# Decode attention backward: whole-head stores move from GpSimd to ScalarE, and o and dq leave in small parts

## The chip, the cores and the metric

The kernel runs on one core of one Trainium2 chip. A core has five engines with a queue of instructions each: TensorE (PE in the profile; its weight loads are PEld), VectorE (DVE), ScalarE (ACT), GpSimd (POOL) and SyncE (SP), which here only issues DMAs. Sixteen DMA engines move data between the HBM and the core's SBUF. The time is device microseconds of one execution; the figure given for a kernel is the median of its runs. A profile is one further execution, and its span runs from the first instruction to the last.

## The reference: what is computed

Attention with one query per head, forward and backward, for 64 heads (batch 2 x 32), 8192 keys and head size 128, all in bfloat16:

```python
scores = jnp.einsum("bhqd,bhkd->bhqk", q, k) * scale
p = _softmax(scores, axis=-1)
return jnp.einsum("bhqk,bhkd->bhqd", p, v)
...
_out, _vjp = jax.vjp(_f, q, k, v)
_grads = _vjp(grad_out)
```

Results are o (out_0), dq (out_1), dk (out_2) and dv (out_3). With dS the gradient of the scores, dk is an outer product of dS and q, and dv one of p and grad_out. So for every head the kernel reads K and V, 2 MB each, and writes dk and dv, 2 MB each; o and dq are 16 KB for all heads together.

## The kernel before

K or V of a head is one tile, [128, 64, 128], with 64 key rows of 256 bytes, one after another, in each of 128 partitions: a transfer of 128 runs of 16 KB. SBUF holds twelve such tiles, six heads. dv of a head is written over its V tile and dk over its K tile, in place; when the tile has been stored, a tile of the head six later is loaded into it. `slot_of` (L80) swaps the two kinds: K of head i + 6 goes where V of head i was, since V is done first.

The program is one long, unrolled list. The loop at L487 goes over slots, eight per head (`SL`), and each slot holds steps of up to four heads. In slot r of a head (`at` and `within` pick the head for which a step is due):

- r = 0 to 7: `transpose_chunk` (L213) turns 16 key rows with eight TensorE transposes into one of two PSUM buffers (`tp`, L220), and ScalarE copies them out (`ev`, L222); r = 0 to 3 for K, 4 to 7 for V. One slot later `score_chunk` (L225) multiplies the copy by the query's window (`raw`, L241). The windows are written by ScalarE (`window`, L194) in slots 1 and 5.
- r = 4 to 12: the score rows are spread over the partitions, the maximum is taken, the exponential (ScalarE, L303) and the sums follow.
- r = 8 to 11 and 12 to 15: `acc` (L390) accumulates o and dq on TensorE.
- r = 9 to 12: `outer` (L450) writes dv into the V tile, a quarter a slot (VectorE, L456); r = 13 to 16: the same for dk.

When `outer` has written the last quarter, it issues the store (L474), on GpSimd, whose DMAs are software DMAs (queue q0 in the profile): GpSimd itself writes their descriptors. For the last head each quarter is stored by itself, on SP. Five heads (6, 18, 30, 42, 54; `SPREAD`) have their K tile stored in two pieces, of 126 partitions and of 2 (`by_rows`, L85). One slot after a store of V, and one after a store of K, the loop calls `load` (L92) for the tile of the head six later; loads go out on SP, as hardware DMAs (queue q1).

`pin` keeps each engine's instructions in the order in which the code writes them. Waits are not written by hand: the framework gives each instruction the semaphores that it must wait for, and each DMA a semaphore that it raises when it has landed. A DMA's wait is made by the engine that issues it, in its place in that engine's queue.

At the start q and grad_out are loaded (L116), the first six rows of q by GpSimd (L112). At the end (L558 to L563) dq and then o, both gathered in SBUF with one column per head, are transposed, copied by VectorE (`nat`, L562) and stored on SP with one DMA each.

Of the kernel before, what the change touches and what calls it, by code (L numbers as in the profile page):

```python
# [11 lines left out]
BF16 = mybir.dt.bfloat16  # L12
# [6 lines left out]
SG = 4  # L19
SW = 32  # L20
NTILE = 12
FIRST = 6
SPREAD = range(6, 60, 12)

@with_exitstack
def kernel(
# [11 lines left out]
    nc = tc.nc  # L39
    B, H, Sq, D = q.shape  # L40
    Sk = k.shape[2]
    P = nc.NUM_PARTITIONS
    assert Sq == 1 and D == P
    BH = B * H
    assert BH <= P
    NT = Sk // P
    assert NT * P == Sk and NT % CH == 0
    NCH = NT // CH
# [1 line left out]
    scale = float(D) ** -0.5  # L50

    load_eng = nc.sync
    store_eng = nc.gpsimd
    pin = tc.keep_in_program_order

    const = ctx.enter_context(tc.tile_pool(name="const", bufs=1))
# [6 lines left out]
    ps_m = ctx.enter_context(tc.tile_pool(name="ps_m", bufs=1, space=bass.MemoryType.PSUM))  # L63
# [12 lines left out]
            self.qb = [None, None]  # L76

    heads = [Head() for _ in range(BH)]

    def slot_of(i, w):  # L80

        n = 2 * i + w
        return n if n < NTILE else slot_of(i - NTILE // 2, 1 - w)

    def by_rows(eng, dst, src, rows):  # L85

        p = 0
        for m in rows:
            pin(eng.dma_start(out=dst[p : p + m], in_=src[p : p + m], max_dma_last_dim=NT * D))
            p += m  # L90

    def load(i, w, pieces=(NCH,)):  # L92
        h = heads[i]
        t = kvp.tile([P, NT, D], BF16, tag=f"kv{slot_of(i, w)}", name="kvt")
        h.tile[w] = t
        src = (v_v if w else k_v)[i]
        c = 0
        for m in pieces:
            n0, n1 = c * CH, (c + m) * CH
            pin(load_eng.dma_start(out=t[:, n0:n1, :], in_=src[:, n0:n1, :]))  # L100
            c += m
# [3 lines left out]
    qd_nat = evp.tile([P, CH, P], BF16, tag="ev", name="qd_nat")  # L105
    for w, a in enumerate((q, grad_out)):
        rows = a.rearrange("b h s d -> (b h s) d")
        r0 = FIRST if w == 0 else 0
        if r0:
            pin(store_eng.inc_swdge_sem([], [], mode="reset_dge_cursor"))  # L110
            pin(
                store_eng.dma_start(  # L112
                    out=qd_nat[:r0, w, :], in_=rows[:r0], max_dma_last_dim=D
                )
            )
        pin(load_eng.dma_start(out=qd_nat[r0:BH, w, :], in_=rows[r0:BH]))  # L116

    load(0, 1)
    for j in range(1, min(NTILE // 2, BH)):
# [22 lines left out]
    for g in range(SG):  # L142
        nc.vector.tensor_copy(
            out=sel4[g * SW : (g + 1) * SW, :, g // 2, :],
            in_=ident_f[g * SW : (g + 1) * SW, g * SW : g * SW + 2 * NCH].rearrange(
                "p (c t) -> p c t", t=2
            ),
# [9 lines left out]
    for w in range(2):  # L157
        nc.vector.tensor_copy(
            out=qd_pair[:BH, w],
            in_=qd_nat[:BH, w, :]  # L160
# [4 lines left out]
        for e in range(2):  # L165
            tps = ps_m.tile([P, BH], BF16, tag=f"acc{e}", name="tps")
# [8 lines left out]
    for w in range(2):  # L175
        tps = ps_m.tile([P, BH], BF16, tag=f"acc{w}", name="tps")
# [3 lines left out]
    dqT = const.tile([P, BH], BF16)  # L180
    oT = const.tile([P, BH], BF16)

    def begin(i):

        h = heads[i]
        sw = ps_sdp.tile([P, 2 * NT + 2 * P + 4], F32, tag="s", name="sw")
        h.score = (sw[:, 0:NT], sw[:, NT : 2 * NT])
        h.s, h.dp = h.score
        h.mT = sw[0:1, 2 * NT : 2 * NT + P]
        h.qbp = sw[:, 2 * NT + P : 2 * NT + 2 * P]  # L190
        h.lsum = sw[:, 2 * NT + 2 * P : 2 * NT + 2 * P + 2]
        h.mb = sw[:, 2 * NT + 2 * P + 2 : 2 * NT + 2 * P + 3]

    def window(i, w):  # L194

        pin(nc.scalar.copy(out=qwin[:, w, :, Q0 : Q0 + 2], in_=qpair[:, w, i]))
# [16 lines left out]
    def transpose_chunk(i, c):  # L213
        w, c = divmod(c, NCH)
        src = heads[i].tile[w]
        tp = ps_tp.tile([P, CH // 2, P], F32, tag="tp", name="tp")
        for m in range(CH // 2):
            n0 = c * CH + 2 * m
            two = src[:, n0 : n0 + 2, :].rearrange("p n d -> p (n d)").bitcast(F32)
            pin(nc.tensor.transpose(tp[:, m, :], two, ident_f[:]))  # L220
        ev = evp.tile([P, CH // 2, P], F32, tag="ev", name="ev")
        pin(nc.scalar.copy(out=ev[:], in_=tp[:]))  # L222
        return ev
# [226 lines left out]
    def outer(i, w, c, ends):  # L450

        h = heads[i]
        n0 = c * CH
        shape = [P, CH, D // 2, 2]
        pin(
            nc.vector.tensor_tensor(  # L456
                out=h.tile[w][:, n0 : n0 + CH, :].rearrange("p n (e t) -> p n e t", t=2),
                in0=h.qb[w][:]
                .rearrange("p (e t) -> p e t", t=2)
                .unsqueeze(1)  # L460
                .to_broadcast(shape),
                in1=h.pair[w][:, n0 : n0 + CH, :].unsqueeze(2).to_broadcast(shape),
                op=ALU.mult,
            )
        )
        if c + 1 in ends:
            at = ends.index(c + 1)
            b0, b1 = (ends[at - 1] if at else 0) * CH, (c + 1) * CH
            dst = (dv_v if w else dk_v)[i]
            if w == 0 and i in SPREAD:  # L470
                by_rows(store_eng, dst, h.tile[w], (P - 2, 2))
            else:
                eng = load_eng if len(ends) > 1 else store_eng
                pin(eng.dma_start(out=dst[:, b0:b1, :], in_=h.tile[w][:, b0:b1, :]))  # L474

    A1 = NCH + 4
    O1 = A1 + 1
    A0 = A1 + NCH
    O0 = A0 + 1
    whole = [NCH]  # L480
    last = list(range(1, NCH + 1))
    AHEAD = NTILE // 2
# [4 lines left out]
    for g in range(SL * BH + O0 + NCH + 4 - SL):  # L487
        now = [(g // SL - b, g % SL + b * SL) for b in range(4)]
        now = [(i, r) for i, r in now if 0 <= i < BH]

        def at(r0):

            return next((i for i, r in now if r == r0), None)

        def within(r0):

            return next(((i, r - r0) for i, r in now if r0 <= r < r0 + NCH), None)

        if (i := at(O1 + NCH)) is not None and i + AHEAD < BH:
            load(i + AHEAD, 0)  # L500
        if (i := at(O0 + NCH)) is not None and i + AHEAD < BH:
            load(i + AHEAD, 1)
        if x := within(O1):
            outer(x[0], 1, x[1], last if x[0] == BH - 1 else whole)
        if x := within(O0):
            outer(x[0], 0, x[1], last if x[0] == BH - 1 else whole)
        ev = None
        if g < SL * BH:
            i, r = divmod(g, SL)
            if r == NCH:  # L510
                begin(i)
                broadcast(i, 1)
            if r == NCH + 2:
                broadcast(i, 0)
            ev = transpose_chunk(i, r)
        if (i := at(A1 + NCH + 2)) is not None:
            join(i, 1)
        if (i := at(A0 + NCH + 2)) is not None:
            join(i, 0)
        if x := within(A1):  # L520
            acc(x[0], 1, x[1])
        if x := within(A0):
            acc(x[0], 0, x[1])
        if (i := at(NCH + 1)) is not None:
            spread_rows(i, 0)
        if (i := at(SL + 1)) is not None:
            spread_rows(i, 1)
        if (i := at(NCH + 3)) is not None:
            max_spread(i)
            expo(i)  # L530
        if prev is not None:
            score_chunk(*prev)
        prev = (g // SL, g % SL, ev) if ev is not None else None
        if (i := at(NCH + 1)) is not None and i + 1 < BH:
            window(i + 1, 0)
        if (i := at(1)) is not None and i > 0:
            window(i, 1)

        if (i := at(NCH)) is not None:
            keep_raw(i)  # L540
        if (i := at(SL)) is not None:
            keep_raw(i)
        if (i := at(NCH + 1)) is not None:
            max_part(i)
        if (i := at(NCH + 2)) is not None:
            max_all(i)
        if (i := at(NCH + 4)) is not None:
            normalise_p(i)
        if (i := at(SL + 1)) is not None:
            weigh(i)  # L550
        if (i := at(SL + 2)) is not None:
            normalise_ds(i)
        if (i := at(A1 + NCH)) is not None:
            pick(i, 1)
        if (i := at(A0 + NCH)) is not None:
            pick(i, 0)

    for w, (src, dst) in enumerate(((dqT, out_1), (oT, out_0))):  # L558
        tps = ps_m.tile([BH, P], BF16, tag=f"acc{w}", name="tps")
        nc.tensor.transpose(tps[:], src[:], ident_bf)  # L560
        nat = evp.tile([P, CH, P], BF16, tag="ev", name="nat")
        nc.vector.tensor_copy(out=nat[:BH, 0, :], in_=tps[:])  # L562
        load_eng.dma_start(out=dst.rearrange("b h s d -> (b h s) d"), in_=nat[:BH, 0, :])  # L563

# [28 lines left out]
```

## Time and profile before

| what | us |
|---|---|
| median of 3 runs (lowest, highest) | 1272.13 (1270.76, 1272.67) |
| the profiled execution: span, which is all that it gives of its own time | 1270.2 |
| TensorE busy in it | 1189.4 (94%) |
| VectorE busy | 1030.9 (81%) |
| ScalarE busy | 557.0 (44%) |
| GpSimd busy | 72.9 (6%) |
| HBM read and written | 268.47 MB each, 423 GB/s over the span |
| issues of SP: tile loads of 2 MB | 127, about 20 to landing (median) |
| issues of GpSimd: whole stores of 2 MB | 121, 49.3 to landing (median) |

How to read it: "busy" counts the time in which an engine executes, and engines work side by side, so shares don't add up to one. "To landing" is the time from a DMA's issue to its completion, queueing included. The page also has the span in 40 equal slices, with the busy share of each engine in tenths, the mean busy share of the DMA engines and what they moved; a list of DMA queues; and a list of waits, which puts each wait of an engine down to what ended it.

### The profile page before, as it was taken

The page shows a single profiled execution, that of the slowest core. Times are in us where ns is not written, and L with a number is a line of the kernel's source. Part 1 is how long each engine was busy: PE and PEld are TensorE (multiplying, and loading weights), DVE is VectorE, ACT ScalarE, POOL GpSimd, SP SyncE. Part 2 cuts the span into 40 slices and gives each one's busy share as a digit, 9 for nine tenths or more (in the row PEclk, how much of TensorE's full clock was granted, in tenths as well). Part 3 has the DMA queues.
Part 4 walks back from the last instruction along what each step waited for, and adds up shares of the span by engine and source line. Part 5 has one row for each costly group of instructions (what it writes and reads, how often), then busy time and mean ns, then how long its engine had stood idle before and what let it go on. Part 6 is the DMA issues. An engine that isn't in the chain of part 4 may idle for free.

```text
span 1270.2 us, 24551 instructions
## 1 busy us (share of the span) xinstructions
PE 1189.4 (94%) x10056; PEld 784.5 (62%) x10056; DVE 1030.9 (81%) x2267; ACT 557.0 (44%) x769; POOL 72.9 (6%) x138
## 2 busy tenths in 40 slices
PE   6999999999999999999999999999999999999991
PEld 4666666666666666666666666666666666565650
DVE  3888888888888888888888888888888888887882
ACT  3444444444444444444444444444444444444430
POOL 0000000000000000000000000000000000000000
PEclk9999999999999999999999999999999999999995
DMA  9999999999999999999999999999999999999997
GB/s 391 418 430 430 430 428 428 431 429 429 429 430 429 430 428 429 427 432 429 428 423 425 431 429 429 428 430 429 425 429 429 428 430 428 429 426 425 429 424 300
DMA packets 39501, 538.53 MB, mean 424 GB/s; under 512 B 4956, under 2 KB 4956, under 8 KB 6236
## 3 DMA queue, kind: packets, MB, share of 16 engines
q1 hardware_dynamic: 20172, 272.70, 50.4%
q0 software_dynamic: 19216, 264.25, 49.0%
q8 instruction: 79, 1.29, 0.4%
q14 instruction: 34, 0.28, 0.1%
HBM read 268.47 MB, written 268.47 MB: 423 GB/s over the span
## 4 chain that ended last, share of the span: by engine, by line
PE 70%; DVE 15%; DMA 9%; another core or an unknown queue 2%; issue 2%; ACT 0%; SPq 0%; POOL 0%; DVEq 0%; ACTq 0%
PE tp L220 30%; PE acc L401 17%; PE raw L241 11%; DVE kvt L456 6%; PE sw L261 4%; DMA out_dram<-kvt 4%; DVE sel L424 4%; DMA kvt<-in_v_dram 3%; DVE rows L254 3%; PE sw L347 3%; PE sw L202 2%; DMA kvt<-in_k_dram 2%; PE sw L285 1%; DVE sel L418 1%
## 5 line engine op out<-in xcount | busy, mean ns | idle before, releaser
L222 ACT COPY ev<-tp 128x1024 f32<-128x1024 f32 x512 | 518.5, 1013 | 661.8 <-PE tp L220 656.3
L456 DVE TENSOR_TENSOR kvt<-qb,pair 128x2048 bf16<-128x2048 bf16 x512 | 616.9, 1216 | 0.1
L220 PE MATMUL tp<-ident_f,kvt 128*128 128x128 f32 x4096 | 548.2, 277 | 3.9 <-DMA kvt<-in_v_dram 3.1
L220 PEld LDWEIGHTS tp<-ident_f,kvt 128*128 128x128 f32 x4096 | 454.5, 144 | 84.9 <-issue 65.9
L241 PE MATMUL raw<-ev,qwin 128*32 128x512 bf16 x2048 | 209.9, 400 | 0.0
L401 PE MATMUL acc<-kvt,dS_pad 128*64 128x512 bf16 x1024 | 160.8, 395 | 0.1
L401 PE MATMUL acc<-kvt,E_pad 128*64 128x512 bf16 x1024 | 160.3, 393 | 0.6 <-DVE E_pad L312 0.6
L261 PEld LDWEIGHTS sw<-sel,rows 128*128 128x128 f32 x1024 | 123.9, 191 | 52.3 <-DVE sel L424 25.9
L424 DVE SCALAR_TENSOR_TENSOR sel<-acc,diag,sel 128x128 f32<-128x128 f32 x384 | 134.7, 351 | 13.6
L241 PEld LDWEIGHTS <-qwin 128*32 128x32 bf16 x2048 | 52.8, 93 | 135.3 <-issue 131.0
L261 PE MATMUL sw<-sel,rows 128*128 128x16 f32 x1024 | 136.3, 265 | 0.0
L474 POOL DMA_DIRECT2D out_dram<-kvt x121 | 64.7, 534 | 1109.9 <-DVE qb L211 545.5
L254 DVE COPY rows<-raw 128x512 f32<-128x512 f32 x128 | 88.5, 692 | 47.9 <-PE raw L241 47.9
L280 DVE TENSOR_REDUCE st<-sw 1x1 f32<-1x128 f32 x64 | 17.9, 279 | 55.9 <-PE sw L279 55.9
L202 PE MATMUL sw<-ident_f,qT 128*128 128x128 bf16 x128 | 28.9, 226 | 36.0 <-DVE st L275 36.0
L401 PEld LDWEIGHTS <-dS_pad 128*64 128x64 bf16 x1024 | 36.7, 109 | 34.4 <-issue 32.1
L347 PEld LDWEIGHTS sw<-st,ones 128*128 128x128 f32 x256 | 38.2, 188 | 30.8 <-issue 15.6
L401 PEld LDWEIGHTS <-E_pad 128*64 128x64 bf16 x1024 | 36.2, 108 | 33.6 <-issue 31.5
L347 PE MATMUL sw<-st,ones 128*128 128x1 f32 x256 | 49.1, 261 | 0.0
L438 PEld LDWEIGHTS acc<-ones,sel 128*128 128x128 f32 x256 | 39.3, 194 | 7.2 <-DVE sel L424 7.2
L418 DVE TENSOR_SCALAR sel<-acc,diag 128x128 f32<-128x128 f32 x128 | 43.7, 341 | 0.0
L438 PE MATMUL acc<-ones,sel 128*128 128x1 f32 x256 | 36.9, 214 | 6.1 <-DVE sel L424 6.1
(53 smaller groups left out, 373.0 us busy)
## 6 DMA issues: line engine op xcount, KB each, us to landing
out_dram<-kvt POOLq DMA_DIRECT2D x121, 2048.0 KB, 49.3
kvt<-in_v_dram SPq DMA_DIRECT2D x64, 2048.0 KB, 20.1
kvt<-in_k_dram SPq DMA_DIRECT2D x63, 2048.0 KB, 20.3
out_dram<-kvt POOLq DMA_DIRECT2D x5, 2016.0 KB, 53.7
out_dram<-kvt SPq DMA_DIRECT2D x8, 512.0 KB, 23.2
kvt<-in_k_dram SPq DMA_DIRECT2D x2, 512.0 KB, 4.4
kvt<-in_k_dram SPq DMA_DIRECT2D x1, 1024.0 KB, 6.9
out_dram<-kvt POOLq DMA_DIRECT2D x5, 32.0 KB, 53.1
```

The source lines that it names most:

```text
L220: pin(nc.tensor.transpose(tp[:, m, :], two, ident_f[:]))
L222: pin(nc.scalar.copy(out=ev[:], in_=tp[:]))
L241: nc.tensor.matmul(h.raw[g * SW : (g + 1) * SW, :], lhsT=qwin[:, w, e, q0 : q0 + SW], rhs=cols[:, b, :, e], start=(c == 0), stop=(c == NCH ...
L254: pin(nc.vector.tensor_copy(out=h.rows[:], in_=h.raw[:]))
L261: nc.tensor.matmul(h.score[w].rearrange("p (n m t) -> p n m t", m=QT, t=2)[:, :, m, :], lhsT=h.rows[:, m * P : (m + 1) * P], rhs=sel4[:].r ...
L347: nc.tensor.matmul(out, lhsT=ones[:].to_broadcast([P, P]), rhs=col, start=True, stop=True)
L401: nc.tensor.matmul(h.acc[w][g : g + CW, :], lhsT=wts[:, n0 : n0 + CW], rhs=rows[:, n0 : n0 + QT, :].rearrange("p n d -> p (n d)"), start=( ...
L418: nc.vector.tensor_scalar(out=h.sel[:], in0=block, scalar1=diag[:, 0:1], scalar2=None, op0=ALU.mult)
L424: nc.vector.scalar_tensor_tensor(out=h.sel[:], in0=block, scalar=diag[:, b : b + 1], in1=h.sel[:], op0=ALU.mult, op1=ALU.add,)
L438: nc.tensor.matmul(h.acc[w][:, 0:1], lhsT=h.sel[:], rhs=ones[:], start=True, stop=True)
L456: nc.vector.tensor_tensor(out=h.tile[w][:, n0 : n0 + CH, :].rearrange("p n (e t) -> p n e t", t=2), in0=h.qb[w][:] .rearrange("p (e t) -> ...
L474: pin(eng.dma_start(out=dst[:, b0:b1, :], in_=h.tile[w][:, b0:b1, :]))
```

## The change

All stores of whole heads go to ScalarE's hardware queue. `outer` no longer issues them but notes them in `pending`; the loop takes that list at the start of the next slot and issues it (`store`) after that slot's transposes and copy, followed by the loads of that slot, which stood at the slot's start before. No head is stored in two pieces any more, and q is loaded in one DMA on SP. The last head's quarters stay on SP. At the end o comes first, on ScalarE, in five DMAs of 11 to 14 rows, and then dq, on SP, in ten DMAs of 2 to 10 rows; `by_rows` no longer pins them.

```diff
-FIRST = 6
-SPREAD = range(6, 60, 12)
+O_ROWS = (11, 12, 13, 14, 14)
+DQ_ROWS = (2, 3, 4, 5, 6, 7, 8, 9, 10, 10)
...
-    store_eng = nc.gpsimd
+    store_eng = nc.scalar
...
+    pending = []
...
         for m in rows:
-            pin(eng.dma_start(out=dst[p : p + m], in_=src[p : p + m], max_dma_last_dim=NT * D))
+            eng.dma_start(out=dst[p : p + m], in_=src[p : p + m])
...
-        r0 = FIRST if w == 0 else 0
-        if r0:
-            pin(store_eng.inc_swdge_sem([], [], mode="reset_dge_cursor"))
-            pin(
-                store_eng.dma_start(
-                    out=qd_nat[:r0, w, :], in_=rows[:r0], max_dma_last_dim=D
-                )
-            )
-        pin(load_eng.dma_start(out=qd_nat[r0:BH, w, :], in_=rows[r0:BH]))
+        pin(load_eng.dma_start(out=qd_nat[:BH, w, :], in_=rows))
...
-            if w == 0 and i in SPREAD:
-                by_rows(store_eng, dst, h.tile[w], (P - 2, 2))
+            if len(ends) > 1:
+                pin(load_eng.dma_start(out=dst[:, b0:b1, :], in_=h.tile[w][:, b0:b1, :]))
             else:
-                eng = load_eng if len(ends) > 1 else store_eng
-                pin(eng.dma_start(out=dst[:, b0:b1, :], in_=h.tile[w][:, b0:b1, :]))
+                pending.append((dst, h.tile[w]))
+
+    def store(due):
+
+        for dst, t in due:
+            pin(store_eng.dma_start(out=dst, in_=t[:]))
...
-        if (i := at(O1 + NCH)) is not None and i + AHEAD < BH:
-            load(i + AHEAD, 0)
-        if (i := at(O0 + NCH)) is not None and i + AHEAD < BH:
-            load(i + AHEAD, 1)
+        due, pending[:] = pending[:], []
...
             ev = transpose_chunk(i, r)
+        store(due)
+        if (i := at(O1 + NCH)) is not None and i + AHEAD < BH:
+            load(i + AHEAD, 0)
+        if (i := at(O0 + NCH)) is not None and i + AHEAD < BH:
+            load(i + AHEAD, 1)
...
-    for w, (src, dst) in enumerate(((dqT, out_1), (oT, out_0))):
-        tps = ps_m.tile([BH, P], BF16, tag=f"acc{w}", name="tps")
+    for w, (src, dst, parts) in enumerate(((oT, out_0, O_ROWS), (dqT, out_1, DQ_ROWS))):
+        tps = ps_m.tile([BH, P], BF16, tag=f"acc{1 - w}", name="tps")
...
-        load_eng.dma_start(out=dst.rearrange("b h s d -> (b h s) d"), in_=nat[:BH, 0, :])
+        by_rows(
+            load_eng if w else store_eng, dst.rearrange("b h s d -> (b h s) d"), nat[:BH, 0, :], parts
+        )
```

## The prediction

> **What bounds the kernel now.** I read the page's slices first, then the queue table, then the waits of SP's queue, and last the transfers of single stretches.
>
> ```profile
> DMA  9999999999999999999999999999999999999997
> GB/s 391 418 430 430 430 428 428 431 429 429 429 430 429 430 428 429 427 432 429 428 423 425 431 429 429 428 430 429 425 429 429 428 430 428 429 426 425 429 424 300
> ...
> q1 hardware_dynamic: 20172, 272.70, 50.4%
> q0 software_dynamic: 19216, 264.25, 49.0%
> ...
> SPq L100 <- DMA out_dram<-kvt: 1126.3, 116, 28.4
> ```
>
> The 16 DMA engines are full from the first slice to the last but one; loads (q1) and stores (q0) share them half and half. The last line says that SP, which loads, nearly always waits for the store that frees the tile. So the sum of the transfers sets the end, as long as every engine has work to the last. The last slice (300 GB/s) shows where that fails.
>
> **The floor.** A 16 KB packet of q1 takes 612.8 ns on average in the trace. A tile of 2 MB is 8 packets on each of 16 engines: 8 x 612.8 = 4.90 us (428 GB/s, as in the row). 256 tiles are 1254.5 us; the first packet starts at 1.8, so evenly loaded engines would be done at 1256.3. In the trace the last packet ends at 1268.2, lands at 1268.8, and the span ends 1.4 us later, at 1270.2. The median run, 1272.13, lies 1.9 above that span, and I add the same 1.9 below.
>
> **The compute's own pace.** The chain of waits has the same product (DVE, L456) at 324.67 and 837.88, 27 heads apart: 19.008 us a head, 9.50 a store. A load and a store together cost the engines 9.80. TensorE thus runs ahead of the transfers by 0.3 us a store, and the stores queue up. These are the transfers of two stretches, 40 to 150 us and 700 to 1000 us (last column: us to landing):
>
> ```profile
> out_dram<-kvt POOLq DMA_DIRECT2D x11, 2048.0 KB, 17.5
> kvt<-in_k_dram SPq DMA_DIRECT2D x5, 2048.0 KB, 42.9
> kvt<-in_v_dram SPq DMA_DIRECT2D x5, 2048.0 KB, 42.8
> ...
> out_dram<-kvt POOLq DMA_DIRECT2D x31, 2048.0 KB, 58.6
> kvt<-in_v_dram SPq DMA_DIRECT2D x15, 2048.0 KB, 19.8
> ```
>
> Late in the run six stores are under way (58.6 / 9.80). GpSimd can afford that: it issues and has nothing else to do.
>
> **What a store can be made to wait for.** The first issues of SP's queue:
>
> ```profile
> 4.76 0.48 SPq L100 DMA_DIRECT2D kvt<-in_k_dram  x1
> 5.99 0.33 SPq L100 DMA_DIRECT2D kvt<-in_v_dram  x1
> 8.61 0.33 SPq L100 DMA_DIRECT2D kvt<-in_k_dram  x1
> ...
> 13.67 0.33 SPq L100 DMA_DIRECT2D kvt<-in_v_dram  x1
> 18.55 0.33 SPq L100 DMA_DIRECT2D kvt<-in_k_dram  x1
> 23.46 0.33 SPq L100 DMA_DIRECT2D kvt<-in_v_dram  x1
> ```
>
> No tile has to come free here, yet SP pauses. The semaphores tell why: the hardware DMAs take eight (100, 110, 111, 112, 113, 114, 117, 118) in turn, and a DMA that reuses one starts when the DMA eight places earlier has landed: 5.97, 8.59, 13.65, 18.54 and 23.45 are the landings. GpSimd's software DMAs go round eight of their own (101 to 108). **My choice:** the stores, once they are hardware DMAs, join the loads in one round of eight, in the order in which the code writes them.
>
> **The change, part by part.**
>
> *Stores to ScalarE.* GpSimd loses 121 whole stores of 0.53 us (64.7 busy) and ten split ones of 0.69; nobody waited for them. ScalarE gains 126 issues, at SP's 0.33 to 0.58 us each: about 1 us per head of 19, in two slots, beside 10 us in which it idles before L222 (661.8 over 64 heads). Cost nothing while that idle time covers it; without it, 1 us a head, 64 us. "One slot later": GpSimd issued at 199.35, as the product's last part ended; ScalarE will issue after the copy of the next slot:
>
> ```profile
> 198.51 1.01 ACT L222 COPY ev<-tp 128x1024 f32<-128x1024 f32 x1 [0.82 <-PE tp L220]
> 200.65 1.01 ACT L222 COPY ev<-tp 128x1024 f32<-128x1024 f32 x1 [1.12 <-PE tp L220]
> 201.56 0.20 ACT L196 COPY qwin<-qpair 128x4 bf16<-128x4 bf16 x1
> ```
>
> So the product is always done and that wait costs nothing; the store leaves 2.4 us later (a slot, 19.008 / 8), hidden by the transfers queued ahead of it. The loads stand behind it on SP, which waits for that store anyway.
>
> *The added wait.* Store number n (V of head 0 is 0, K of head 0 is 1) is followed in the code by load 12 + n. Stores and loads alternate, so eight places before store n is store n - 4: four stores may be under way, 4 x 9.5 = 38 us. Stores that take 17.5 us pass; at 58.6 they would not. Behind a waiting store in ScalarE's order are the copies that empty the transpose banks (L222, two buffers) and the window copies (L196). TensorE needs the copy of 198.51 only at 202.03, so 2 us of lateness are free, and then the whole compute stands still. While it only slows TensorE to 9.80 a store, this loses nothing: the engines stay full.
>
> *The end of the loads.* Load 127 follows store 115 (K of head 57). After it stores come alone, and the place eight before changes kind: store 116 waits for store 112, but **store 117 (K of head 58) waits for load 124**, a load that could start only when store 112 had landed. Rings of equal share, four stores (113 to 116) and four loads (121 to 124) in them: both finish together, at 125 loads + 117 stores = 242 tiles, 1.8 + 242 x 4.90 = 1187.6. Lower bound: two loads in flight, as from 700 to 1000 (19.8 us): two tiles less, 1177.8. I take the upper end: the early stretch (42.8 us, over four loads) is the one without a split store before it; what shortened the loads later are the split stores, which go (next part). Unhindered, store 117 would be due at 47.29 (first K store) + 58 x 19.008 + 2.4 = 1152.1. So ScalarE stands for up to 36 us, part of it spread over the slow stores before.
>
> *From there to the end.* In the trace the last product ends at 1244.96, of which 5.2 are load waits (1046.96 to 1223.26 is 176.3 instead of 9 x 19.008 = 171.1). From K of head 58 that is 1244.96 - 5.2 - 1149.7 - 2.4 = 87.7 us. New end of the products: 1187.6 + 87.7 - 2.0 (free lateness) = 1273.3. By then the stores are almost drained: the compute ends the kernel, no longer the transfers.
>
> *o and dq in parts.* Before:
>
> ```profile
> 1247.93 3.39 SPq L563 DMA_DIRECT2D out_dram<-nat  x2
> ```
>
> dq left SP 3.0 us after the last product, and both landed behind the big stores, free of charge. Now dq's ten parts stand in the open: SP's first issues follow each other at 0.50 (eight from 0.74 to 4.76), so the tenth starts at 1273.3 + 3.0 + 9 x 0.5 = 1280.8, lands 1.7 later (1.0 from issue to first packet at the start of the trace, 0.6 from last packet to landing at its end), 1282.5. o's five on ScalarE go earlier. The price is 4.5 us, at least 3 (0.33 each); nothing if the stores still cover them.
>
> *None special.* The six rows of q on GpSimd and the five split heads go. In the trace the landings of one store's 16 engine shares lie 3.4 us apart at 160 us, 23 at 460, 40 at 950; the growth falls at the split heads. Even engines would be worth up to 1268.2 - 1256.3 = 11.9 us, 9 if 3 us of spread stay: a gain only where the transfers set the end. Software packets of 16 KB average 615.9 ns instead of 612.8: 8 x 121 x 3.1 ns = 3.0 us, in those 11.9. q in one piece: within 1 us either way, since the last product (1244.96) lies 11 us ahead of the floor.
>
> **Two rules.** The Trainium skill (DMA: Bandwidth & Descriptors, Issuing engines are not separate DMA queues) says that DMAs of all issuing engines share the same 16 engines, and that another issuer saves only its sequencer's time. That agrees with 50.4% and 49.0% above and speaks against a gain from the move: by it the sum is 1272. The same page (Latency and other measured facts) guesses that descriptor rings of software DMAs slow engines 7 and 15; by it the even engines of the first rival come, 1268. The trace does not name the engines.
>
> **Sum.** 1282.5 + 1.4 = span 1283.9, against 1270.2; with 1.9: 1285.8. I say 1285. Its own range is 1277 to 1292: 1177.8 instead of 1187.6 gives 1276; 3 us of spread in the landing, or a slow restart of TensorE, adds to it.
>
> **Rivals.**
> - *The engines even out and nothing stands still* (ScalarE's stores get a round of their own, or the loads fall three places later, so that no late store has a load eight before it). For it: GpSimd has its own eight. Products end at 1248; transfers at 1256.3 + 3 = 1259.3; dq's third part waits for the last big store eight places ahead (the 2.4 us that o's issue waited in the trace are such a wait), then 7 x 0.5 + 1.7 + 1.4: span 1266.5, run 1268 (1262 without spread or o/dq price, 1271 with more). This is the other side; it decides if ScalarE's longest wait stays under 20 us. 0.28.
> - *The wait is shorter*: two loads in flight, or loads one place later: 1276 (1271 to 1280). 0.17.
> - *The wait comes all along*: stores meet loads in the round from the start and the engines run dry: 1300. 0.07.
> - *The forecast*: 0.48.
>
> A measurement of this kernel can tell about 0.2% from no change: 1269.6 to 1274.7. Faster: 0.7 of the first rival, 0.20. Same: the rest of it and a quarter of the second, 0.12. Slower: 0.68. The range takes in most of the first rival and the forecast's own: 1264 to 1293.
>
> **What would show it.** Right: in ScalarE's waits one of 20 to 36 us on a load, near 1150 to 1188, TensorE idle with it; store landings near 39 us before; the last slices well under 400 GB/s, the last product near 1273, dq's issues after it. Wrong: no wait of ScalarE on a DMA, stores at 58 us to landing, and the last big store later than dq's first part. A landing spread of 10 us or more without split heads would break the first rival's gain.

## The result and the profile after

The changed kernel takes 1304.17 us (median of 4 runs, 1303.99 to 1304.54) against 1272.4 for the kernel before on the same chip: 1.0246 of its time, 95% interval 1.0231 to 1.026. The prediction was 1285, slower for the reason that came true, but 19 us short and outside its range. The profiled execution has a span of 1302.2 us (before: 1270.2).

The page of the changed kernel, busy share of the DMA engines, what they moved, and the two queues (q10 is ScalarE's):

```profile
DMA  9999999999999999999999999999999999999756
GB/s 394 419 430 429 429 429 429 429 430 427 430 428 430 429 429 428 431 427 430 428 430 428 431 428 431 428 431 425 426 427 425 424 426 429 424 426 381 306 224 260
...
q1 hardware_dynamic: 20160, 272.69, 49.5%
...
q10 hardware_dynamic: 18272, 264.27, 47.7%
```

The engines are full up to slice 36 (1172 us) as before, and then four slices lie between 224 and 381 GB/s; before, only the last one was low. The waits of the changed kernel (us in total, times, longest), ScalarE's and then, in a row of its own, those of SP's queue, nearly what they were before:

```profile
ACT qwin L189 <- DVE st L273: 107.6, 25, 4.3
ACT qwin L189 <- DVE dS_pad L380: 90.1, 22, 4.1
...
ACT qwin L189 <- DMA kvt<-in_k_dram: 34.0, 2, 26.0
...
ACT qwin L189 <- DMA out_dram<-kvt: 12.9, 5, 4.9
```

```profile
SPq L101 <- DMA out_dram<-kvt: 1114.3, 115, 24.0
```

L189 is the window copy, the first instruction behind a store in ScalarE's order: what it waits for is the store's wait. The first two rows name VectorE, which had long been done; 47 waits of some 4 us cannot be its doing. The store itself waited, for the store four places ahead, which from 640 us on lands 39.8 us after its issue. The third row is the stop at the end. It is this place in ScalarE's timeline (start, length, in brackets the idle time before and what ended it):

```profile
1207.60 0.34 ACTq L471 DMA_DIRECT2D out_dram<-kvt  x1
1207.98 0.19 ACT L189 COPY qwin<-qpair 128x4 bf16<-128x4 bf16 x1 [26.02 <-DMA kvt<-in_k_dram]
```

In this trace the DMAs of SP and of ScalarE take the same eight semaphores in turn (101 to 106, 109, 110); by its semaphore this is store 117, and load 124 landed at 1207.52. From there the compute runs free to its end:

```profile
1291.67 2.35 DVE L449 TENSOR_TENSOR kvt<-qb,pair 128x2048 bf16<-128x2048 bf16 x2
...
1294.43 2.58 ACTq L90 DMA_DIRECT2D out_dram<-nat  x5
...
1296.99 3.35 SPq L90 DMA_DIRECT2D out_dram<-nat  x10
```

The last product ends at 1294.0 (before: 1245.0), o and dq follow, and the span ends at 1302.2.

**One engine is slower than the others.** The landing that came 20 us late pointed at single DMA engines. The trace has the time of every packet. Of the 29,919 packets of 16 KB between 50 and 1200 us, 27,893 took 611 ns and 1,838, which is 0.98 of a sixteenth, took 627.3 on average. An engine's packets follow each other 4 ns before the former one's end, so they can be followed back from a landing: the share that lands last is made of the slow packets (8 of its last 8, in the kernel of experiment 2 below), the other 15 of fast ones. So one engine takes 16 ns more for each packet, some 2.5 us per 100 us. The kernel before has it too (1,902 slow packets, 1.04 of a sixteenth). These are the landings of the 16 shares of one store, in us behind the first:

```
changed, store at 896:          0 .1 .4 .5 .7  9.6 13.5 13.6 13.6 13.7 13.9 15.5 15.6 15.8 15.9  27.4
before without cuts, at 925:    0 .2 .3 .8 1.2 4.4  9.3  9.5  9.6  9.7  9.7 10.2 10.4 11.6 11.8  24.7
before, at 950:                 0 16.9 19.0 19.9 20.9 22.1 24.7 26.6 35.9 36.7 36.8 37.2 37.7 38.0 38.2 38.3
```

In the first two rows one share is far behind the rest. In the third one share is far ahead, and nothing is alone at the end. At the very end of the kernel of the second row the slow engine can be seen by itself: from 1271.3 to 1280.9 us its packets are the only big ones left.

### The profile page after: what moved, and what is told of

It reads as the page before. It is cut to its first block, busy times and chain, and to the rows that moved or that the text cites. A ratio compares the mean times of both kernels' runs of the same rounds, so it can differ in the third digit from the quotient of the medians.

```text
span 1302.2 us, 24548 instructions
## 1 busy us (share of the span) xinstructions
PE 1197.1 (92%) x10056; PEld 789.9 (61%) x10056; DVE 1028.9 (79%) x2267; ACT 550.1 (42%) x769; POOL 0.7 (0%) x6
## 4 chain that ended last, share of the span: by engine, by line
PE 65%; DVE 17%; DMA 10%; ACT 4%; issue 2%; ACTq 1%; SPq 0%
PE tp L213 27%; PE acc L394 15%; PE raw L234 11%; DVE kvt L449 6%; DMA kvt<-in_k_dram 5%; PE sw L254 4%; DMA out_dram<-kvt 4%; DVE sel L417 4%; ACT ev L215 4%; DVE rows L247 3%; PE sw L340 3%; PE sw L195 2%; DVE sel L411 1%; PE acc L431 1%; PE sw L272 1%
## 5 line engine op out<-in xcount | busy, mean ns | idle before, releaser
L215 ACT COPY ev<-tp 128x1024 f32<-128x1024 f32 x512 | 512.9, 1012 | 457.2 <-PE tp L213 457.0
L234 PEld LDWEIGHTS <-qwin 128*32 128x32 bf16 x2048 | 57.3, 93 | 180.5 <-issue 174.8
L189 ACT COPY qwin<-qpair 128x4 bf16<-128x4 bf16 x128 | 25.1, 196 | 270.3 <-DVE st L273 107.6
L204 DVE CAST qb<-sw 128x128 bf16<-128x128 f32 x128 | 36.2, 283 | 32.4 <-PE sw L195 32.4
L305 DVE CAST E_pad<-E_f 128x64 bf16<-128x64 f32 x64 | 12.5, 195 | 46.6 <-ACT E_f L296 46.6
```

Source lines behind the costliest of these rows:

```text
L204: pin(nc.vector.tensor_copy(out=h.qb[w][:], in_=h.qbp))
L234: nc.tensor.matmul(h.raw[g * SW : (g + 1) * SW, :], lhsT=qwin[:, w, e, q0 : q0 + SW], rhs=cols[:, b, :, e], start=(c == 0), stop=(c == NCH ...
```

## The experiments

The theory after the result: (a) stores and loads share one round of eight semaphores, so ScalarE stands still for store n - 4, and at the end for load 124; (b) the slow engine sets the landings, and the cut stores of the kernel before had relieved it. Each experiment's time is the median of its runs, with the ratio to the kernel before on the same chip.

### 1. Is it ScalarE that stands? (e1, e4)

```diff
-                pending.append((dst, h.tile[w]))
+                pending.append((i, dst, h.tile[w]))
...
-        for dst, t in due:
-            pin(store_eng.dma_start(out=dst, in_=t[:]))
+        for i, dst, t in due:
+            eng = load_eng if i >= BH - AHEAD else store_eng
+            pin(eng.dma_start(out=dst, in_=t[:]))
```

> The changed kernel, but the stores of heads 58 to 63 are issued by SP, which has no load left to issue by then; the wait on load 124 stays, on an engine that computes nothing. The theory (ScalarE, standing at store 117 behind load 124, holds the compute back, and the compute then ends the kernel): ScalarE's stop of 26 us is gone, products from head 58 on come one every 9.5 us from store 115 on, so the last product ends near 1272 (in the changed kernel store 116 leaves at 1175.6 and ScalarE restarts at 1207.6; without the stop the compute of that point restarts 28 us sooner), and the run takes 1278 to 1288. First rival (the transfers end the kernel anyway, the stop is hidden): 1302 to 1306. Second rival (o and dq in parts are the cost): the same, 1300 or more.

Measured: 1288.81 us, ratio 1.0136 [1.0121, 1.0151], 15.4 less than the changed kernel and just above what was expected. The wait for load 124 is now made by SP. ScalarE's longest wait for a load, and the last product and dq in the timeline:

```profile
ACT qwin L189 <- DMA kvt<-in_k_dram: 7.6, 1, 7.6
```

```profile
1267.21 2.35 DVE L449 TENSOR_TENSOR kvt<-qb,pair 128x2048 bf16<-128x2048 bf16 x2
...
1279.41 5.44 SPq L90 DMA_DIRECT2D out_dram<-nat  x10
```

The last product ends at 1269.6 (24 us earlier; expected 1272), but the last big packet only at 1283.3: the transfers end the kernel again. With the slow engine as it is, the stop at the end is worth 15.4 us and no more.

The second kernel of this group stores dq and then o whole, on SP, as before:

```diff
-    for w, (src, dst, parts) in enumerate(((oT, out_0, O_ROWS), (dqT, out_1, DQ_ROWS))):
-        tps = ps_m.tile([BH, P], BF16, tag=f"acc{1 - w}", name="tps")
+    for w, (src, dst) in enumerate(((dqT, out_1), (oT, out_0))):
+        tps = ps_m.tile([BH, P], BF16, tag=f"acc{w}", name="tps")
...
-        by_rows(
-            load_eng if w else store_eng, dst.rearrange("b h s d -> (b h s) d"), nat[:BH, 0, :], parts
-        )
+        load_eng.dma_start(out=dst.rearrange("b h s d -> (b h s) d"), in_=nat[:BH, 0, :])
```

> The changed kernel, but dq and then o stored whole by SP at the end, as in the kernel before. The theory (ten parts of dq, 0.34 us apart in SP's queue after the last product, are a cost of 3 to 4.5 us, the rest of the loss lies before the last product): 1299 to 1302. The rival (small parts are what costs, by waiting for semaphores of earlier DMAs): most of the 32 us goes, 1275 to 1285.

Measured: 1302.47 us, ratio 1.0243 [1.0228, 1.0259], half a microsecond above the range of the theory and far from the rival. By the medians the parts cost 1.7 us, by the ratios to the kernel before (1.0246 and 1.0243) 0.4: under 2 us, and not clear of noise.

### 2. What were the cuts worth? (e3, e11, e15, e16)

First the kernel before without them:

```diff
-SPREAD = range(6, 60, 12)
+SPREAD = ()
```

> The kernel before, with its stores on GpSimd, but no head stored in two pieces. The theory (equal shares leave one engine behind, whoever issues): the spread of the landings grows to 20 us or more and never falls, the last stores land late, 1277 to 1290. The rival (the growth comes from two hardware queues, or the split stores make the spread in the kernel before): the spread stays small, 1262 to 1273.

Measured: 1284.86 us, ratio 1.0105 [1.0088, 1.0122]: 12.8 us slower, with every whole-head store still on GpSimd. The lag of the last share behind the first grows evenly, by some 2.7 us per 100 us, to 30.2 for the store of 1124 us. The last big packet ends at 1280.9 (before: 1268.1). That is the slow engine's own work: 256 tiles x 8 packets x (627.2 - 4) ns + 1.8 = 1278.1, and a few longer packets.

Then with the cuts, but with all of q loaded by SP:

```diff
-FIRST = 6
+FIRST = 0
...
+        if w == 0:
+            pin(store_eng.inc_swdge_sem([], [], mode="reset_dge_cursor"))
         if r0:
-            pin(store_eng.inc_swdge_sem([], [], mode="reset_dge_cursor"))
```

> The kernel before with its five cut stores, but all of q loaded by SP, so that GpSimd's DMAs start from the first engine. Theory (the six rows choose which two engines the cuts spare): the slow engine is not spared, gets one row more at each cut, and the landings spread to 30 us as without cuts: 1284 to 1290. Rival (the cuts help whichever engines they spare): 1270 to 1274.

Measured: 1297.91 us, ratio 1.0192 [1.0175, 1.0209]. The same five cuts now make the kernel 13 us slower than none: the share of slow packets lands 56 us behind the first. That is above the expected 1284 to 1290; why 13 and not the 3 of five added rows is not settled.

Two more pin it down: the K stores cut in 120 and 8 rows, with nine rows behind them so that each cut starts at the same engine, and six or five rows of q on GpSimd:

```diff
-                by_rows(store_eng, dst, h.tile[w], (P - 2, 2))
+                by_rows(store_eng, dst, h.tile[w], (P - 8, 8))
+                pin(
+                    store_eng.dma_start(
+                        out=out_0.rearrange("b h s d -> (b h s) d")[:9],
+                        in_=ident_f[:].bitcast(BF16)[:9, :D],
+                        max_dma_last_dim=D,
+                    )
+                )
```

> The kernel before, with each of the five K stores cut on GpSimd in 120 and 8 rows instead of 126 and 2, and a small store of 9 rows of a constant to out_0 behind it (overwritten by o at the end), so that every cut starts from the same engine. Theory: 120 rows spare one engine, the sixth with six rows of q ahead, by 8 rows, and no other engine gets a row more from them. If the sixth is the slow one: 1266 to 1271, up to 3 us (5 x 0.61) less than before. If it is the fifth: it gets its full share, and the run takes 1280 to 1290, as without cuts. Rival (which engines are spared does not matter): 1270 to 1274.

> The same with five rows of q on GpSimd instead of six, so that the 120 rows spare the fifth engine. Theory: the opposite of its twin: 1266 to 1271 if the fifth engine is the slow one, 1280 to 1290 if it is the sixth. Rival: 1270 to 1274.

Measured: with six rows 1294.7 us, ratio 1.0166 [1.0148, 1.0185]; with five 1273.61, ratio 1.0003 [0.9992, 1.0014]. What the engines moved in each slice, with six rows and then with five:

```profile
GB/s 393 422 430 429 430 427 429 429 430 428 429 429 425 427 425 428 426 429 428 424 407 418 428 430 428 428 428 419 416 428 429 429 428 429 421 417 410 430 408 152
```

```profile
GB/s 391 423 429 431 428 429 429 430 427 430 429 428 426 427 429 429 428 429 429 429 415 420 429 430 428 429 429 429 426 428 428 429 428 430 428 428 428 429 428 286
```

One row of 256 bytes at the start of the program decides 21 us. Around 910 us the last share of a store lands 26 us behind the one before it with six rows, 1.5 us with five. The Trainium skill (DMA: Bandwidth & Descriptors, Why a DMA increments its semaphore by 16 and not by 1) says that a DMA uses the largest number of engines, up to 16, that divides its rows (some software copies excepted, which use all 16), that hardware DMAs take the lowest-numbered ones and software DMAs go on from a round-robin cursor. Counted that way, 120 rows spare the sixth engine with six rows of q ahead and the fifth with five, so the slow one is the fifth. The trace gives no engine a name, but which of the four kernels take long agrees with this count.

The sizes agree less well. The run with five rows was expected at 1266 to 1271 and came out in the rival's range (which engines are spared does not matter: 1270 to 1274); it is the 1294.7 of its twin that rules this rival out. And the twin should have been as slow as no cuts, 1284.86, and is 10 us slower, as the one without rows of q is 13 slower. So five cuts that do not relieve the slow engine cost 10 us or more; why, and whether cuts that relieve it pay this too, stays open.

### 3. Is it the shared round? (e7)

```diff
-            pin(load_eng.dma_start(out=t[:, n0:n1, :], in_=src[:, n0:n1, :]))
+            eng = nc.gpsimd if i >= NTILE // 2 else load_eng
+            pin(eng.dma_start(out=t[:, n0:n1, :], in_=src[:, n0:n1, :]))
...
+    pin(nc.gpsimd.inc_swdge_sem([], [], mode="reset_dge_cursor"))
```

> The changed kernel, with the loads from head 6 on issued by GpSimd, as software DMAs with semaphores of their own; stores stay on ScalarE and no head is cut. The theory (ScalarE waits because its stores and SP's loads share one round of eight; with a round of stores alone, store n waits for store n - 8): ScalarE's waits on DMAs shrink from some 270 us to under 20, and what is left is the slow engine: 1282 to 1291, near the kernel before without cut stores (1284.9). Rival (issuing the stores on ScalarE costs by itself): 1295 or more.

Measured: 1285.8 us, ratio 1.0105 [1.009, 1.012]: 18.4 us less than the changed kernel, with the stores still on ScalarE and no cut. The longest wait of ScalarE's window copy is now at the start, for VectorE, and none is for a DMA:

```profile
ACT qwin L191 <- DVE qpair L169: 9.6, 2, 8.6
```

The last big packet ends at 1279.2, again the slow engine's time, and the run is within 1 us of the kernel before without cuts (1284.86). So issuing on ScalarE costs nothing that can be seen here; sharing the round does. (The loads also changed their queue, from SP's to GpSimd's; what that is worth by itself was not measured.)

### 4. Does relief of the slow engine help the changed kernel?

Cuts made with hardware DMAs came first: both pieces (126 and 2 rows) on ScalarE; the 2 rows on GpSimd, which keeps the number of hardware DMAs; that with the tail on SP as well; and in the kernel before 120 and 8 rows on ScalarE.

```diff
+SPREAD = range(6, 60, 12)
...
+            split = w == 0 and i in SPREAD
+            for a, b in ((0, P - 2), (P - 2, P)) if split else ((0, P),):
+                pin(store_eng.dma_start(out=dst[a:b], in_=t[a:b]))
```

> The changed kernel, with the K stores of heads 6, 18, 30, 42 and 54 cut in two DMAs again, of 126 and 2 rows, both on ScalarE. The theory (one of the 16 engines falls behind at about 2.5 us per 100 us under equal shares, and the landing of every DMA is that engine's; the cut stores relieved it): if that engine is one of those which a DMA of 126 rows leaves out, the spread of the landings falls by some 20 us at each cut store or stays under 10, load 124 lands near 1188 instead of 1207.5, and the run takes 1280 to 1290. If it is another engine, or the growth comes from ScalarE's and SP's queues running side by side: 1302 to 1308, with the spread at 20 to 27 us as before.

> The changed kernel, with the K stores of heads 6, 18, 30, 42 and 54 cut: 126 rows on ScalarE, the last 2 rows on GpSimd. The number and order of the hardware DMAs stay those of the changed kernel; only one or two engines get 8 packets less at each cut. In the traces one engine takes some 627 ns for a 16 KB packet where the others take 611, and it is the one that lands last. The theory (that engine's 31 us set the landings; it is among those that 126 rows spare, 5 x 8 x 0.61 = 24 us): load 124 lands between 1186 and 1194 instead of at 1207.5, ScalarE's 4 us at every store from 640 us on go, the last product falls from 1293 to some 1273 to 1280, and the run takes 1284 to 1292. Rival (the unevenness costs nothing; the waits of ScalarE are a matter of the order alone): 1300 to 1306.

> The kernel of the split with the 2 rows on GpSimd, and the stores of heads 58 to 63 on SP. The theory (two causes, ScalarE's stop behind load 124 and the slow engine, and they add up): both gone, the transfers end the kernel again, 1268 to 1278. Rival (they are one cause, undoing either is all that there is to win): 1284 to 1290, as with the tail on SP alone.

> The kernel before, with the five K stores cut in 120 and 8 rows, both issued by ScalarE as hardware DMAs (only loads are in that round of eight), instead of 126 and 2 by GpSimd. The theory says that one engine needs relief and no other: if 120 rows spare that engine, and it alone, the landings of a DMA stay within some 8 us and the run takes 1258 to 1269, less than before. If 120 rows do not spare it: 1282 to 1290, as without any cut. Rival (cut stores help by something other than the slow engine's share): 1270 to 1275, as before.

Measured: 1314.67 [ratio 1.0322 to 1.0352], 1320.98 [1.0345, 1.04], 1311.1 [1.0248, 1.0317] and 1303.01 [1.0224, 1.0254]. All four missed what I expected. By the count of group 2 a hardware DMA of 126 or 120 rows spares the last engines, and the slow one, the fifth, gets rows on top; that these engines are the ones is argued, not shown. The first and the last also brought new waits, as an added DMA shifts the round so that ScalarE waits for loads; ScalarE's waits in the first of them, and in the last:

```profile
ACT qwin L190 <- DMA kvt<-in_v_dram: 74.2, 8, 13.9
ACT qwin L190 <- DMA kvt<-in_k_dram: 21.2, 5, 7.3
```

```profile
ACT ev L222 <- DMA kvt<-in_k_dram: 58.2, 4, 18.6
```

How much of the loss is the rows and how much the waits was not told apart.

Then cuts on GpSimd, with the six rows of q ahead as in the kernel before: a cut K store as a quarter on ScalarE and three quarters on GpSimd, so that the round keeps its order; and the same with the tail on SP.

```diff
+FIRST = 6
+SPREAD = range(4, 58, 7)
...
+            cut = w == 0 and i in SPREAD
+            n = CH if cut else NT
+            pin(store_eng.dma_start(out=dst[:, :n, :], in_=t[:, :n, :]))
+            for a, b in ((0, P - 2), (P - 2, P)) if cut else ():
+                pin(nc.gpsimd.dma_start(out=dst[a:b, n:, :], in_=t[a:b, n:, :], max_dma_last_dim=NT * D))
```

> The changed kernel, with the slow engine relieved as the kernel before does it, and the order of the hardware DMAs kept: the first six rows of q loaded by GpSimd again, and the K stores of eight heads (4, 11 to 53) stored as a quarter by ScalarE and the other three quarters by GpSimd in 126 and 2 rows. Theory, mended after the cuts made with hardware DMAs did not relieve the slow engine: software DMAs go on from the engine at which the last one ended; six rows first, so 126 rows spare the engines after the fourth and the fifth, and the slow one is among these two; a hardware DMA always spares the last ones. Eight cuts take 8 x 7 x 12 KB from it, 25 of its 31 us. So load 124 lands at 1186 to 1195 instead of 1207.5, the 4 us waits of ScalarE at every store go or come late, and the run takes 1282 to 1292. Rival (the landing of load 124 does not depend on the slow engine): 1300 to 1306. If the two engines spared are others: 1304 to 1312.

> The same, with the stores of heads 58 to 63 on SP. Theory (the slow engine and ScalarE's stop behind load 124 are two causes): 1268 to 1279. Rival (one cause; the tail on SP alone gave 1288.8): 1284 to 1290.

Measured: 1292.05 us, ratio 1.0153 [1.0138, 1.0168], and 1293.55, ratio 1.0174 [1.0152, 1.0195]. In the first, load 124 lands at 1194.9 instead of 1207.5, the stores land after some 20 us instead of 39.8, and the last product ends at 1279.9, 14 us earlier: as expected, at the upper end. But at the cuts a store and a load changed places in the round, and ScalarE waited there for loads:

```profile
ACT qwin L199 <- DMA kvt<-in_v_dram: 36.5, 6, 8.7
...
ACT qwin L199 <- DMA kvt<-in_k_dram: 7.2, 1, 7.2
```

With the tail on SP as well, nothing more was gained, and 1293.55 lies outside both its theory and its rival. That these waits hold the compute back by themselves is the likely reason, but it was not tested, so the second kernel is no answer. Cutting loads instead of stores (a quarter on SP, the rest on GpSimd) leaves the order alone:

```diff
+FIRST = 6
+CUT = range(8, 60, 7)
...
+            cut = w == 0 and i in CUT
+            n2 = n0 + CH if cut else n1
+            pin(load_eng.dma_start(out=t[:, n0:n2, :], in_=src[:, n0:n2, :]))
+            for a, b in ((0, P - 2), (P - 2, P)) if cut else ():
+                pin(nc.gpsimd.dma_start(out=t[a:b, n2:, :], in_=src[a:b, n2:, :], max_dma_last_dim=NT * D))
```

> The changed kernel; the slow engine is relieved in the loads this time. The six rows of q on GpSimd again, and the K loads of eight heads (8, 15 to 57) as a quarter by SP and three quarters by GpSimd in 126 and 2 rows. Stores and hardware DMAs keep their number and alternate as in the changed kernel, so no new waits of ScalarE at the cuts (the kernel with cut stores had 44 us of them on loads). Theory: load 124 lands at 1185 to 1197 instead of 1207.5, ScalarE's waits at every store from 640 us on shrink below 2 us each, the stop at store 117 to 20 us or less; last product 1270 to 1281; 1282 to 1292. Rival (the landing of load 124 does not depend on the slow engine): 1300 to 1306.

> The same, with the stores of heads 58 to 63 on SP. Theory (two causes that add up: ScalarE's stop for the last loads, and the slow engine, which makes it wait for stores and lands last at the end): with both gone the transfers end the kernel, 1265 to 1277. Rival (one cause, for the tail on SP alone gave 1288.8): 1282 to 1290.

Measured: 1299.55 us, ratio 1.0213 [1.0195, 1.0231], a miss: load 124 lands at 1202.9, and stores still take 39.7. The slow engine was relieved (the last share of load 124 lands 1.2 us behind the one before it, in the changed kernel 16.4), but other packets became slower. In stretches of 20 us that hold packets of a cut load, 3.8 sixteenths of the 16 KB packets are slow, in all others 0.98; with the cut stores above it was 0.96 and 0.97. Why cut loads do this is open. With the tail on SP: 1281.39, ratio 1.007 [1.0055, 1.0085]; last product 1264.5, last big packet 1274.9. That is just below the rival's range and above the theory's, 7.4 us less than the tail on SP alone, and its packets end 6 us before the 1280.9 at which the slow engine is done with a full share. So relief and tail are two causes, and they add (4.6 and 15.4 us alone, 22.8 together), but the relief brought far less than I had reckoned.

### 5. Closing the sum

Two kernels with the loads on GpSimd and cuts as well, first of loads, then of stores (all on GpSimd), were to come back to 1272:

```diff
+            if w == 0 and i in CUT:
+                for a, b in ((0, P - 2), (P - 2, P)):
+                    pin(nc.gpsimd.dma_start(out=t[a:b, n0:n1, :], in_=src[a:b, n0:n1, :], max_dma_last_dim=NT * D))
+            else:
+                eng = nc.gpsimd if i >= NTILE // 2 else load_eng
+                pin(eng.dma_start(out=t[:, n0:n1, :], in_=src[:, n0:n1, :]))
...
+            if w == 0 and i in SPREAD:
+                for a, b in ((0, P - 2), (P - 2, P)):
+                    pin(nc.gpsimd.dma_start(out=dst[a:b], in_=t[a:b], max_dma_last_dim=NT * D))
```

> The changed kernel with loads from head 6 on by GpSimd, and five K loads (heads 8, 20, 32, 44, 56) cut in 126 and 2 rows after the six rows of q, as the kernel before cuts its stores. Stores on ScalarE, one slot later, o and dq in parts as in the changed kernel. Theory (all of the loss is the shared round and the missing cuts): 1266 to 1276, within 4 us of the kernel before. Rival (something else in the change costs 10 us or more): 1280 to 1290.

> The changed kernel with loads from head 6 on by GpSimd, six rows of q by GpSimd first, and the K stores of heads 6, 18, 30, 42 and 54 cut in 126 and 2 rows on GpSimd; other stores stay on ScalarE. Its twin with cut loads took 1287 because its loads came to take 50 to 66 us and the compute ended the kernel at 1279; here the cuts are on stores, as in the kernel before. Theory (the loss is the shared round and the slow engine, nothing else): the loads stay below 25 us, the slow engine is spared 21 of its 29 us, and the run takes 1268 to 1278. Rival (something else in the change costs 10 us or more): 1283 to 1290.

Measured: 1287.19 us, ratio 1.0117 [1.0102, 1.0133], and 1304.86, ratio 1.0243 [1.0226, 1.0261]. Both missed. The transfers of the first from 700 to 1000 us (last column: us to landing):

```profile
kvt<-in_v_dram POOLq DMA_DIRECT2D x15, 2048.0 KB, 64.9
kvt<-in_k_dram POOLq DMA_DIRECT2D x14, 2048.0 KB, 65.0
```

Without the cuts these loads took 15.7. A cut transfer goes in packets of 8 KB, the others in 16 KB, and the two queues alternate packet by packet in the trace: while a cut passes, the other queue gets ahead (that this is the cause is argued; the landings fit it). Cut stores let the loads ahead (before: 42.8 us to landing until 150 us, 29 after the first cut, 16.5 after the second), cut loads the stores. With late loads the compute is late: the last product ends at 1278.9 and not at 1245. In the second kernel GpSimd issued no load from 184.6 to 220.1, until the first cut store had landed at 219.4; its later loads take 58 us (median). So neither closes the sum. The last one comes from the other side: stores back on GpSimd, cut as before; the later slot and the small parts stay.

```diff
-            pin(store_eng.dma_start(out=dst, in_=t[:]))
+            cut = w == 0 and i in SPREAD
+            for a, b in ((0, P - 2), (P - 2, P)) if cut else ((0, P),):
+                more = {"max_dma_last_dim": NT * D} if cut else {}
+                pin(nc.gpsimd.dma_start(out=dst[a:b], in_=t[a:b], **more))
```

> The changed kernel with its whole-head stores back on GpSimd, six rows of q there first, and the K stores of heads 6, 18, 30, 42 and 54 cut in 126 and 2 rows as in the kernel before. What stays of the change: stores and loads issued one slot later, o and dq in parts (o on ScalarE). Theory (the loss is the round shared with the loads and the slow engine, which the move to ScalarE brought; the rest costs next to nothing while the big stores cover it): 1270 to 1276. Rival (the rest of the change costs, by the later slot or the small parts): 1278 or more.

Measured: ratio 1.0029 [1.0008, 1.0049], 1275.11 us; last product 1245.4, last big packet 1269.6. The rest of the change costs 2.7 us, by the interval 1.0 to 6.2.

## Why the prediction was wrong

**What was right.** The round of eight, shared by the loads and the stores, and its order: store 117 waited for load 124, the first place where the kind changes. The stop: 26.0 us, forecast 20 to 36. The engines no longer full after it, and the compute as the end: from the landing to the last product the forecast has 87.7 - 2.0 = 85.7 us, and the trace 1294.0 - 1207.5 = 86.5. That the kernel gets slower.

**The step that failed** is "both finish together, at 125 loads + 117 stores = 242 tiles, 1.8 + 242 x 4.90 = 1187.6". It landed at 1207.5; these 20 us are the error, and what the other terms missed nearly cancels. The number of tiles held: 125 loads and 116 stores had landed by then, and the next store was under way. The price of a tile did not. The 4.90 is the mean over 16 engines, but a DMA has landed when its last share has. For the slow engine it is 242 x 8 x (627.3 - 4) ns + 1.8 = 1208.6. The pace shows it as well: with 16 slow packets a store and a load take 16 x 623.3 ns = 9.97 us and not 9.80, and the late stores leave ScalarE every 9.97.

**Why it was missed** is the part "None special". It read the spread of the landings, growing to 40 us at the cut heads, as unevenness that the cuts make, and counted up to 11.9 us of gain without them. The sign was wrong. The spread grew because the spared engines ran ahead, which costs nothing; taking the cuts away costs 12.8 us (group 2). The rows for it were there: one packet in sixteen of 627 ns in the kernel before, hidden in the mean of 612.8. (Under "The floor", 256 x 8 x 612.8 ns is 1255.0 and not 1254.5; half a microsecond changes nothing here.)

**The first rival** (1268) was given 0.28 as if only ScalarE's wait stood against it. Experiment 3 gives the stores their own round, and takes 1285.8: without cuts the transfers end with the slow engine, at 1279.2 there and 1280.9 in the kernel before without cuts. The sign that the prediction named against this rival, a spread of landings of 10 us or more without split heads, came with 27 us.

**The other terms.** ScalarE's waits all along were a rival at 0.07 with 1300; they did come, 4 us at each store from 640 us on, but the engines stayed full (424 to 431 GB/s), so they cost little by themselves. The o and dq parts were put at 4.5 us, at least 3; they cost under 2: the ten issues are 0.34 apart, not 0.50, and whole ones have a price after the last product too. The move and the later slot at nothing: the last run puts all that is left, the parts in it, at 2.7. Of the 31.8 us, then, 12.8 are the missing cuts (before, with and without) and 18.4 the shared round (changed, with loads in the same round and in another), 15.4 of these at the end; between the two kernels that link them lies 1 us (1284.86 and 1285.8). This is one way through the kernels; undoing the two in the other order was not measured cleanly, since cuts in the changed kernel brought waits of their own.

**The two rules.** The rule (the Trainium skill, DMA: Bandwidth & Descriptors, Issuing engines are not separate DMA queues) that another issuer brings no engines of its own held: in experiment 3 the stores on ScalarE's queue come within 1 us of the kernel before without cuts, neither gain nor loss. The other place of that page (the Trainium skill, DMA: Bandwidth & Descriptors, Latency and other measured facts) guesses that rings of software DMAs slow two engines, the eighth and the last. It does not fit here: the changed kernel has no software DMA at all, and one engine is slow in it as in the others, by the count of group 2 the fifth.

No kernel here beats the kernel before; the one with 120 and 8 rows and five rows of q equals it.

## What to carry to other kernels

Where the DMA engines are full, don't take a landing from the mean packet: look how the times of the packets are distributed, and price a landing by the slowest engine's share. Before odd row counts or a few odd rows are taken out as untidy, find out which engines they spare. And before a DMA is given to an engine that computes, count back the places of its semaphore round, up to the end, where the kinds stop alternating.

## What the hardware showed unexpectedly

- One of the 16 DMA engines takes some 627 ns for a packet of 16 KB, the others 611, in loads and stores, on hardware and software queues, on all five chips that the experiments ran on. The slow packets are 0.94 to 1.08 of a sixteenth in 16 of the 20 kernels; in the four with cut loads, or with loads and cut stores both on GpSimd, they are 1.2 to 1.5, and in the one examined for it (the first with cut loads) the surplus falls where packets of a cut are under way. Why the one engine is slow, these runs do not tell.
- Five or six rows loaded by GpSimd ahead of all its other DMAs made 1273.6 or 1294.7 us, which fits software DMAs that go on from the engine where the last one ended.
- Half-size packets in one queue let the other ahead: loads came down from 42.8 to 16.5 us to landing with two cut stores, and with cut loads they rose to 29 after the first and to 65 late in the run, where uncut ones took 15.7.
